# Two-level products one group earlier: the projection factor's second level prepared inside the first group's projection

## The chip, the cores and the metric

One core of one Trainium2 chip. The metric is device time in microseconds (us) of one execution; the median of several runs is compared. Engines are named as in the profile: PE is TensorE, DVE is VectorE, ACT is ScalarE, POOL is GpSimd, SP is SyncE, which here only issues transfers.

## The reference

An attention block without softmax feeds a gated feed-forward block, all in float32 (`w1` to `w_out` arrive as float64 and are converted on the chip).

```
kv  = einsum('bhsd,bhse->bhde', k, v)          # batch 8, heads 8, seq 576, head_dim 64
o   = einsum('bhsd,bhde->bhse', q, kv)
x   = o / sqrt(mean(o*o, -1) + 1e-6) * g_norm  # rows: 8 x 576 = 4608 tokens, 512 columns
a   = x @ w1                                   # 512 -> 1024
b   = x @ w2                                   # 512 -> 1024
out = ((a * b) @ w3) @ w_out                   # 1024 -> 1024 -> 512
```

## The kernel before

**Folded weights.** `w3 @ w_out` does not depend on the tokens, so the kernel first forms that 1024 x 512 matrix, `w3o_sb`, here called the projection factor (lines 664 to 686, the first 84 us). What is left for each token is: the gates `x @ w1` and `x @ w2`, their product, and one projection by `w3o_sb`.

**Groups.** Tokens are taken in nine groups of 512: T = 0 to 6 hold the first 512 tokens of batches 0 to 6, T = 8 the 64 left-over tokens of all eight batches, and T = 7 those of batch 7; they run in the order 0, 1, ..., 6, 8, 7. "First group" is T = 0, "second" T = 1, and so on. While group T is in its gates and projection, the attention of batch T + 1 is computed in pieces, set between the matmuls by `between()` (lines 1400 to 1418): each call takes one of eight pieces from `steps(T + 1)`. For an odd batch there is one product more, `product_left` (L431), for the left-over tokens of two batches.

**One level.** `winograd` (lines 695 to 735) multiplies two matrices, cut two by two, by seven half-size products instead of eight (the Strassen-Winograd scheme). It needs sums of blocks of the left factor (`sums`: s1 to s4) and differences of blocks of the right one (`combine`: t1 to t4). The gates take it once for each of four pairs of 128-column blocks, p = 0 to 3, for both `w1` and `w2`: 28 matmuls of 128 x 256 at L702 for one p. In the order of the code: the products a11 x b11, s1 x t1, s2 x t2, then `between`, s4 x b22 (block c12 is done), s3 x t3 (c22), a12 x b21 (c11), then `between`, a22 x t4 (c21). Products are collected in PSUM banks, five of which (`ps_mm`) go round; ACT copies (L715, `keep`) and DVE additions (L844, L845) finish the blocks. The copies u2 and u3 share one buffer, so u3 waits until the c12 addition has read u2; the last product is added to the bank that u3 copies, so it waits for u3.

**Two levels.** The same scheme can be used again inside each product. `project_twice` does so for the projection of every group but the first: 98 matmuls of 128 x 128 at L1169 for a group. The first group's projection, `project`, has one level (56 matmuls of 128 x 256 at L702). The factor for the second level is made once, by `prepare_b` (lines 1065 to 1091): seven steps n = 0 to 6, one for each block or block difference of `w3o_sb` (`b_blocks`: b11, t1, t2, b22, t3, b21, t4), each of four DVE subtractions of 128 x 256 (one of them in place) into a stage, and two stores to the DRAM buffer `w3o_l2`; one more store at the start keeps b21 as it was. Groups then load it part by part with `load_b`, in three buffers, `streams`, that lie over `w3o_sb` and the space of its differences; the second group's projection is the first to use it.

In the gates, `gates_of_two` (lines 932 to 1024) takes p = 0 and 1 together in two levels, 98 matmuls of 128 x 128 at L960, for the groups from `FIRST_OF_TWO` = 3 on, that is from the fourth; p = 2 and 3 stay with `winograd`. The second level's sums of the gate weights are made one group ahead, by `prepare_w` and `replace_a21` (lines 875 to 896), called from T = FIRST_OF_TWO - 1: 28 DVE instructions and 18 stores to the DRAM buffer `w_l2`; `load_w` brings them back in five parts for every group in two levels. Their stages (`in_a_row`, lines 798, 799 and 1514) lie in t1's space, in the last row of `w3o_sb` with the end of t4's space, and in a tile of their own.

**Turning.** Attention needs transposes of q and of its result. They go by DMA: a copy that splits the words (L293, L295), a DMA transpose (L297, issued by SP), a copy back (L307). POOL makes these copies up to batch FIRST_OF_TWO - 1, and ACT, in set places (`turns_by_scalar`), from batch FIRST_OF_TWO on.

**What sets the order.** PE, POOL and SP execute in the order in which the code issues. SP therefore also waits in that order: a store that waits for DVE holds back every transfer written after it. The order on DVE and ACT is made by the scheduler from estimated times, with the code's order as priority, except where the code fixes it by hand on DVE (the last gates pass and the projection of a group, and the two-level gates of the last two groups). `tc.issue_after(x)` only says that an instruction comes behind x on its own engine. Both execute their queue strictly in order once it is made.

`combine_x(T)` makes t1 to t4 of a group's x, in the buffer `xc` (and t3 in place). For T = 1 it is called after the first group's projection:

```
        project(T, between)
        run(combine_x(1))
        preparing, preparing_w, prepared, replaced = prepare_b(), prepare_w(), [], []
```

Of the kernel before, what the change touches and what calls it, by code (L numbers as in the profile page):

```python
# [22 lines left out]
def kernel(  # L23
# [32 lines left out]
    nc = tc.nc  # L56
    PSUM = bass.MemoryType.PSUM
    P = 128
# [3 lines left out]
    DF = w1.shape[1]  # L62
    NP = H // 2
    KF = DF // P
    FIRST_OF_TWO = 3
    NH = KF // 2
    J = 4
    G = J * P
# [46 lines left out]
    NF = KF // 2  # L115
# [576 lines left out]
    def late_tile(name):  # L692
        return late_pool.tile([P, 7, P], FP32, name=name[0] if name[0] == "u" else name)

    def winograd(lhsT, rhs, chunks, done, between=lambda: None, keep_u3=True):


        def product(a_name, b_name, to=None):
            ps = to if to is not None else bank(ps_mm, "mm").rearrange("p (u n) -> p u n", u=2)
            for u in range(2):  # L700
                for c in range(chunks):
                    nc.tensor.matmul(  # L702
                        ps[:, u, :],
                        lhsT=lhsT(a_name, u, c),
                        rhs=rhs(b_name, c),

                        start=(u == 0 and c == 0 and to is None),
                        stop=(c == chunks - 1),
                        skip_group_check=True,
                    )  # L710
            return ps

        def keep(name, ps):
            t = late_tile(name)[:, 0:4, :].rearrange("p (u a) n -> p u (a n)", u=2)
            copies.setdefault(name, []).append(nc.scalar.copy(t, ps))  # L715
            run_slot((stage[0], name), copies[name][-1])
            late[name] = t
            return t

        r1 = product("a11", "b11")  # L720
        p1 = keep("p1", r1)
        r2 = product("s1", "t1")
        p5 = keep("p5", r2)
        product("s2", "t2", r1)
        u2 = keep("u2", r1)
        between()
        product("s4", "b22", r2)
        done("c12", r2, u2)
        product("s3", "t3", r1)
        done("c22", p5, keep("u3", r1) if keep_u3 else r1)  # L730
        r3 = product("a12", "b21")
        done("c11", r3, p1)
        between()
        product("a22", "t4", r1)
        done("c21", r1, None)
# [297 lines left out]
            lambda: nc.vector.tensor_sub(s4, c21, s2),  # L1033
        ]

    def project(T, between):
        def done(name, one, two):
            half, j = int(name[1]) - 1, int(name[2]) - 1
            dst = o_sbs[half][:, :, j * N:(j + 1) * N]
            if two is None:  # L1040
                nc.scalar.copy(dst, one)
            else:
                nc.vector.tensor_add(dst, one, two)
            if name in ("c11", "c21"):
                rows = out[T * S:T * S + G, :].rearrange("(p j) f -> p j f", j=J)
                nc.sync.dma_start(out=rows[:, 2 * half:2 * half + 2, :], in_=o_sbs[half])

        winograd(
            lambda name, m, p: aa[p][name][:, m * P:(m + 1) * P],
            lambda name, p: ob[p][name],  # L1050
            NF, done, between,
        )


# [10 lines left out]
    def prepare_b():  # L1065

        nc.sync.dma_start(
            out=w3o_l2[7, :, 0:1024].rearrange("p (f n) -> p f n", n=N), in_=b_blocks()[5]
        )
        for n, y in enumerate(b_blocks()):  # L1070
            b11, b12, b21, b22 = (
                y[:, 2 * i:2 * i + 2, j * P:(j + 1) * P] for i in range(2) for j in range(2)
            )


            stage = w3o_sums[0].rearrange("p f n -> p (f n)") if n == 4 else (
                o_sbs[(n - n // 5) % 2].rearrange("p m n -> p (m n)")
            )
            stage = stage[:, 0:6 * P]
            t1, t2, t4 = (t.rearrange("p (c n) -> p c n", n=P) for t in (  # L1080
                stage[:, i * 2 * P:(i + 1) * 2 * P] for i in range(3)
            ))
            nc.vector.tensor_sub(t1, b12, b11)
            nc.vector.tensor_sub(t2, b22, t1)
            nc.vector.tensor_sub(b12, b22, b12)
            nc.vector.tensor_sub(t4, b21, t2)
            nc.sync.dma_start(
                out=w3o_l2[n, :, 0:1024].rearrange("p (f n) -> p f n", n=N), in_=y
            )
            nc.sync.dma_start(out=w3o_l2[n, :, 1024:PART], in_=stage)  # L1090
            yield
# [5 lines left out]
    def load_b():  # L1097
        n = len(loaded_b)
        if n == ALL_B:
            return  # L1100
        i = n % 7
        t = streams[n % 3] if n < 7 else streams[(i + 1 if i < 3 else i) % 3]
        if n >= 7 and i == 3:
            done_with = xT[groups[1 + n // 7]]
            t = done_with.rearrange("p i j r n -> p (i j r n)")[:, 0:PART]

        part = {ALL_B - 2: 6, ALL_B - 1: 7}.get(n, n % 7)

        queue = nc.scalar if i in ((3, 5) if n < 7 else (4, 6)) else nc.sync
        if n + 1 < ALL_B:  # L1110
            queue.dma_start(out=t, in_=w3o_l2[part])
        else:
            t = t[:, 0:1024]
            queue.dma_start(out=t, in_=w3o_l2[part, :, 0:1024])
        loaded_b.append(t)
# [275 lines left out]
    for n, T in enumerate(groups):  # L1391
# [8 lines left out]
        def between():  # L1400
            if len(converted) < len(begun):
                with tc.issue_after(copies["u2"][-1].ins):
                    end_next()
            next(pieces, lambda: None)()
            if T == FIRST_OF_TWO - 1 and p == 1 and len(prepared) == 1:
                with tc.issue_after(adds["c21"][-1].ins):
                    prepare_some(2)
            if T == 1:
                late_half = len(adds["c12"]) > len(adds["c21"])
                behind = adds["c21"][-1] if p else adds["norm"]  # L1410
                with tc.issue_after(behind.ins):
                    for _ in range((0 if late_half else 1) if p == 1 else 3 if p == 2 else 2):
                        if next(preparing, 0) == 0 and len(loaded_b) < 3:
                            load_b()
            if T == FIRST_OF_TWO - 1 and p == 2:
                replaced.append(True)
                if len(replaced) == 2:
                    replace_a21()
# [18 lines left out]
        for p in range(NF):  # L1437
# [23 lines left out]
            if T == 0:  # L1461

                def begin_early(behind):
                    t = early.pop(0)
                    with tc.issue_after(behind.ins):
                        next(t)
                    next(t)

                if p == 0:
                    begin_early(copies["xT"])  # L1470
                if p + 1 < NF:
                    ops = sum_w(p + 1)
                    if p != 2:
                        ops.pop(0)()
                    with tc.issue_after(adds["c12"][p].ins):
                        run(ops)
                for n in range(2):
                    if len(converted) < len(todo):
                        ahead = [copies["p5"][p] if p else copies["xT"], copies["u3" if p == 1 else "u2"][p]][n]
                        with tc.issue_after(ahead.ins):  # L1480
                            begin_next()
                        if len(begun) < len(todo):
                            with tc.issue_after(adds["c12"][0].ins):
                                end_next()
                if p == 0:
                    begin_early(copies["u3"][0])
                if p + 1 == NF:
                    allocate_projection()
                    first, *others = zip(*(f(i) for i in range(NF) for f in (sum_ab, combine_w3o)))
                    with tc.issue_after(adds["c21"][p - 2].ins):  # L1490
                        all_of(step() for step in first)
                    with tc.issue_after(adds["c12"][p - 1].ins):
                        all_of(step() for steps in others for step in steps)
            else:
                ops = [step() for step in sum_ab(p)]
                with tc.issue_after(ops[-1].ins):
                    if p == 1:
                        prepare_some(3)
                    if (T, p) == (1, 1):
                        all_of(preparing)  # L1500
        last = n + 1 == NG
        if T:
            project_twice(
# [2 lines left out]
            )  # L1506
            in_order.__exit__(None, None, None)
            continue
        project(T, between)
        run(combine_x(1))  # L1510
        preparing, preparing_w, prepared, replaced = prepare_b(), prepare_w(), [], []
        third = late_pool.tile([P, 3, 2, P], FP32, name="inner_sums")
        inner_sums.append([third[:, i] for i in range(3)])
        in_a_row.append({"s1": third.rearrange("p s c t -> p (s c t)")})
# [30 lines left out]
```

## Time and profile before

| | us |
|---|---|
| median of 3 runs | 749.06 |
| lowest, highest | 748.76, 749.10 |
| the profiled execution | 749.29 |
| its span, from the first to the last instruction | 747.5 |

| engine | busy us | share of the span | instructions |
|---|---|---|---|
| PE, matmuls | 740.4 | 99% | 6759 |
| PE, weight loads (beside matmuls) | 658.8 | 88% | 6759 |
| DVE | 639.6 | 86% | 1339 |
| ACT | 361.8 | 48% | 630 |
| POOL | 40.9 | 5% | 46 |

The profile is of one execution, the last two rows of the first table, and its sums are to be set against that execution's own time. The granted TensorE clock was 1.00. A line such as L702 is the line in the kernel's file. Names in the profile are those of the tiles: `raw` is the space that held the converted weights and later holds the differences of the projection factor, the stages and the outputs; `w3o_l` and `w_l` are the DRAM buffers of the two second levels; `ws` are the sums of the gate weights, `xc` and `xT` the tokens.

### The profile page before, as it was taken

The page shows a single profiled execution, that of the slowest core. Times are in us where ns is not written, and L with a number is a line of the kernel's source. Part 1 is how long each engine was busy: PE and PEld are TensorE (multiplying, and loading weights), DVE is VectorE, ACT ScalarE, POOL GpSimd, SP SyncE. Part 2 cuts the span into 40 slices and gives each one's busy share as a digit, 9 for nine tenths or more (in the row PEclk, how much of TensorE's full clock was granted, in tenths as well). Part 3 has the DMA queues.
Part 4 walks back from the last instruction along what each step waited for, and adds up shares of the span by engine and source line. Part 5 has one row for each costly group of instructions (what it writes and reads, how often), then busy time and mean ns, then how long its engine had stood idle before and what let it go on. Part 6 is the DMA issues. An engine that isn't in the chain of part 4 may idle for free.

```text
span 747.5 us, 16773 instructions
## 1 busy us (share of the span) xinstructions
PE 740.4 (99%) x6759; PEld 658.8 (88%) x6759; DVE 639.6 (86%) x1339; ACT 361.8 (48%) x630; POOL 40.9 (5%) x46
## 2 busy tenths in 40 slices
PE   8999999999999999999999999999999999999998
PEld 6455788888899889999999999999999999999997
DVE  6977998748889877988898989898989997898897
ACT  6687778413322565357636753565367323222321
POOL 0000000133330100010000000100001000000000
PEclk9999999999999999999999999999999999999999
DMA  9997925539998996677967997689659763465354
GB/s 313 361 310 208 265 93 133 125 83 265 278 311 301 277 286 167 228 229 211 305 227 220 228 275 263 209 240 283 234 133 243 203 222 100 154 225 172 130 197 140
DMA packets 134737, 165.32 MB, mean 221 GB/s; under 512 B 77956, under 2 KB 110724, under 8 KB 134660
## 3 DMA queue, kind: packets, MB, share of 16 engines
q1 hardware_dynamic: 132208, 149.84, 66.8%
q10 hardware_dynamic: 2452, 14.42, 5.6%
q8 instruction: 53, 0.87, 0.5%
q14 instruction: 24, 0.20, 0.1%
HBM read 126.22 MB, written 20.71 MB: 197 GB/s over the span
## 4 chain that ended last, share of the span: by engine, by line
PE 92%; DMA 3%; DVE 3%; ACT 1%; issue 0%; SPq 0%; ACTq 0%; DVEq 0%
PE mm L702 40%; PE mm L1169 22%; PE mm L960 18%; PE mm L681 5%; PE at L334 2%; DMA raw<-in_moe_w_dram 2%; PE at L412 1%; DMA raw<-in_moe_w_out_dram 1%; PE mm L412 1%; DMA w3o_sb<-w3o_l 1%; PE at L668 1%; DVE ab L162 1%; DVE w_sb L172 0%; PE at L1220 0%; ACT ab L158 0%
## 5 line engine op out<-in xcount | busy, mean ns | idle before, releaser
L702 PE MATMUL mm<-xT,w_sb 128*128 128x256 f32 x528 | 121.2, 379 | 0.0
L702 PEld LDWEIGHTS mm<-xT,w_sb 128*128 128x128 f32 x528 | 99.5, 190 | 13.5 <-issue 0.5
L702 PE MATMUL mm<-xc,ws 128*128 128x256 f32 x384 | 86.8, 379 | 0.0
L702 PEld LDWEIGHTS mm<-xc,ws 128*128 128x128 f32 x384 | 73.0, 190 | 9.9
L681 PE MATMUL mm<-chunks,ab 128*128 128x512 f32 x128 | 60.4, 604 | 0.7 <-DVE chunks L172 0.7
L715 ACT COPY u<-mm 128x512 f32<-128x512 f32 x42 | 24.6, 586 | 58.7 <-PE mm L702 41.2
L715 ACT COPY p<-mm 128x512 f32<-128x512 f32 x50 | 29.5, 589 | 45.5 <-PE mm L702 30.4
L1180 ACT COPY u<-mm 128x512 f32<-128x512 f32 x23 | 13.5, 586 | 77.8 <-DVE raw L1193 45.8
L1169 PE MATMUL mm<-w3o_sb,ab 128*128 128x128 f32 x368 | 48.7, 275 | 0.0
L1169 PE MATMUL mm<-w3o_sb,raw 128*128 128x128 f32 x372 | 48.1, 275 | 0.2 <-DMA w3o_sb<-w3o_l 0.2
L702 PE MATMUL mm<-xc,w_sb 128*128 128x256 f32 x192 | 46.4, 384 | 0.7 <-ACT u L715 0.7
L960 PE MATMUL mm<-ws,w3o_sb 128*128 128x128 f32 x300 | 46.2, 275 | 0.0
L1169 PEld LDWEIGHTS mm<-w3o_sb,ab 128*128 128x128 f32 x368 | 45.4, 192 | 0.4
L1169 PEld LDWEIGHTS mm<-w3o_sb,raw 128*128 128x128 f32 x372 | 44.7, 192 | 0.4 <-issue 0.4
L702 PE MATMUL mm<-xT,ws 128*128 128x256 f32 x176 | 42.3, 383 | 0.0
L681 PEld LDWEIGHTS mm<-chunks,ab 128*128 128x128 f32 x128 | 21.8, 190 | 23.3 <-issue 15.3
L380 DVE TENSOR_REDUCE inv<-sq 128x8 f32<-128x512 f32 (+1 forms) x40 | 24.3, 628 | 20.2 <-ACT sq L379 20.2
L702 PEld LDWEIGHTS mm<-xc,w_sb 128*128 128x128 f32 x192 | 35.7, 190 | 6.5 <-ACT u L715 1.5
L960 PEld LDWEIGHTS mm<-ws,w3o_sb 128*128 128x128 f32 x300 | 39.8, 192 | 0.0
L702 PEld LDWEIGHTS mm<-xT,ws 128*128 128x128 f32 x176 | 32.9, 190 | 4.7
L839 ACT COPY c<-mm 128x256 f32<-128x256 f32 x24 | 8.9, 370 | 57.0 <-PE mm L702 57.0
L845 DVE TENSOR_TENSOR ab<-c 128x256 f32<-128x256 f32 x72 | 32.5, 452 | 1.9
(244 smaller groups left out, 1685.5 us busy)
## 6 DMA issues: line engine op xcount, KB each, us to landing
w3o_sb<-w3o_l SPq DMA_DIRECT2D x18, 896.0 KB, 6.8
w3o_sb<-w_l SPq DMA_DIRECT2D x18, 896.0 KB, 6.1
raw<-in_moe_w_dram SPq DMA_DIRECT2D x31, 512.0 KB, 7.4
raw<-w3o_l SPq DMA_DIRECT2D x15, 896.0 KB, 4.8
w3o_sb<-w3o_l ACTq DMA_DIRECT2D x14, 896.0 KB, 5.2
k_sb<-in_k_dram SPq DMA_DIRECT2D x16, 576.0 KB, 4.5
v_sb<-in_v_dram SPq DMA_DIRECT2D x16, 576.0 KB, 6.3
q_sb<-in_q_dram SPq DMA_DIRECT2D x32, 256.0 KB, 3.7
```

The costliest lines, as they stand in the source:

```text
L162: nc.vector.scalar_tensor_tensor(out=low_bits, in0=hi, scalar=0x80000000, in1=low_bits, op0=ALU.bitwise_and, op1=ALU.bitwise_or,)
L334: nc.tensor.matmul(ps[r * D:(r + 1) * D, :], lhsT=k_sb[rows, r, cols], rhs=v_sb[rows, r, cols], start=(j == 0), stop=(j == JS - 1),)
L380: adds["norm"] = nc.vector.tensor_reduce(out=inv[:, i], in_=sq.rearrange("p (h d) -> p h d", d=D), axis=AX.X, op=ALU.add)
L412: nc.tensor.matmul(o_ps[l][tokens, n * D:(n + 1) * D], lhsT=qT[r][rows, e, i, tokens], rhs=kv_b[rows, m // 2 ^ l, e, h, :], start=True, st ...
L681: nc.tensor.matmul(sums_ps[half][m], lhsT=w3T[half, c][:, m, :], rhs=chunks[:, c, 1, :], start=(c == 0), stop=(c == KF - 1),)
L702: nc.tensor.matmul(ps[:, u, :], lhsT=lhsT(a_name, u, c), rhs=rhs(b_name, c),  start=(u == 0 and c == 0 and to is None), stop=(c == chunks ...
L715: copies.setdefault(name, []).append(nc.scalar.copy(t, ps))
L839: copied = nc.scalar.copy(c, one[:, 0, :])
L845: nc.vector.tensor_mul(dst, c[:, 0, :], c[:, 1, :])
L960: nc.tensor.matmul(ps[place // 4][:, place % 4, :], lhsT=x, rhs=y, start=new and place // 4 not in seen, stop=True, skip_group_check=True,)
L1169: nc.tensor.matmul(to[:, i, :], lhsT=x[:, c, :], rhs=y[:, c, :], start=new and place // 4 not in seen, stop=(c == 1), skip_group_check=True,)
L1180: nc.scalar.copy(t[:, 0:4], ps[0])
```

## The change

`FIRST_OF_TWO` goes from 3 to 2. So the third group's gates take p = 0 and 1 in two levels, the second group makes the sums of the gate weights for it (`prepare_w`, `replace_a21`), and ACT makes the turning copies of batch 2.

`prepare_b` leaves the second group, where it was set in portions between the passes. It is begun inside the first group's projection: a new argument `after` of `winograd` is called after each product's matmuls, and takes two steps of `prepare_b` after the fourth product and one each after the fifth and sixth. The other three steps come behind the projection. The stages change with it: n = 0 and 1 use `xc`, the others the space of the sums of `ab` (`ab_sums`). `combine_x(1)` is put behind the last addition of the projection's outputs on DVE. The first three loads of the projection factor in the second group are written at one place, at p = 2.

```diff
-    FIRST_OF_TWO = 3
+    FIRST_OF_TWO = 2
...
-    def winograd(lhsT, rhs, chunks, done, between=lambda: None, keep_u3=True):
+    def winograd(
+        lhsT, rhs, chunks, done, between=lambda: None, keep_u3=True, after=lambda: None,
+    ):
...
                         skip_group_check=True,
                     )
+            after()
             return ps
...
-    def project(T, between):
+    def project(T, between, after):
...
-                nc.vector.tensor_add(dst, one, two)
+                adds["out"] = nc.vector.tensor_add(dst, one, two)
...
-            NF, done, between,
+            NF, done, between, after=after,
...
-            stage = w3o_sums[0].rearrange("p f n -> p (f n)") if n == 4 else (
-                o_sbs[(n - n // 5) % 2].rearrange("p m n -> p (m n)")
-            )
-            stage = stage[:, 0:6 * P]
+            if n < 2:
+                stage = xc.rearrange("p s c n -> p (s c n)")[:, n * 6 * P:(n + 1) * 6 * P]
+            else:
+                stage = ab_sums[(n - 2) % 3].rearrange("p f n -> p (f n)")[:, 0:6 * P]
...
-            if T == 1:
-                late_half = len(adds["c12"]) > len(adds["c21"])
-                behind = adds["c21"][-1] if p else adds["norm"]
-                with tc.issue_after(behind.ins):
-                    for _ in range((0 if late_half else 1) if p == 1 else 3 if p == 2 else 2):
-                        if next(preparing, 0) == 0 and len(loaded_b) < 3:
-                            load_b()
+            if T == 1 and p == 2 and not loaded_b:
+                for _ in range(3):
+                    load_b()
...
-                    if (T, p) == (1, 1):
-                        all_of(preparing)
...
-        project(T, between)
-        run(combine_x(1))
-        preparing, preparing_w, prepared, replaced = prepare_b(), prepare_w(), [], []
+        preparing, calls = prepare_b(), []
+
+        def after():
+            for _ in range((0, 0, 0, 2, 1, 1, 0)[len(calls)]):
+                next(preparing)
+            calls.append(True)
+
+        project(T, between, after)
+        with tc.issue_after(adds["out"].ins):
+            run(combine_x(1))
+        all_of(preparing)
+        preparing_w, prepared, replaced = prepare_w(), [], []
```

## The prediction

> **What bounds the kernel now.** I read the busy table first, then the chain that ended last, by engine and in order of time, then windows of whole groups.
>
> ```profile
> span 747.5 us, 16773 instructions
> ...
> PE 740.4 (99%) x6759; PEld 658.8 (88%) x6759; DVE 639.6 (86%) x1339; ACT 361.8 (48%) x630; POOL 40.9 (5%) x46
> ...
> PE 92%; DMA 3%; DVE 3%; ACT 1%; issue 0%; SPq 0%; ACTq 0%; DVEq 0%
> ```
>
> TensorE is busy 99% of the span and carries 92% of the chain: a microsecond off its work, or added to it as a wait, is a microsecond of the kernel. The chain through the third group (T = 2) shows the work (start, duration, what; counts take matmuls and weight loads together):
>
> ```profile
> 240.17 10.36 PE mm L702 x48
> ...
> 252.67 19.19 PE mm L702 x88
> ...
> 274.00 5.38 PE mm L702 x24
> 279.38 0.62 PE at L431 x32
> 280.01 14.01 PE mm L702 x64
> 294.02 21.88 PE mm L1169 x196
> ```
>
> There is no gap: 112 matmuls of 256 columns at L702 in 48.94 us (10.36 + 19.19 + 5.38 + 14.01), the attention of batch 3 between them, 98 matmuls of 128 columns at L1169. The fifth group (T = 4) has the same odd kind of batch in its slots, but takes the gates of p = 0 and 1 in two levels:
>
> ```profile
> 403.31 9.38 PE mm L960 x84
> 412.69 0.62 PE at L431 x32
> 413.31 6.45 PE mm L960 x56
> 419.76 1.09 PE at L412 x64
> 420.85 6.45 PE mm L960 x56
> ```
>
> Here 98 matmuls at L960 (22.28 us) stand for 56 at L702. The windows of the second, third and fifth group (length; busy time of PE, PEld, DVE, ACT, POOL; clock; DMA share; GB/s):
>
> ```profile
> 164.55:240.17 75.62, 75.40 (x694) 68.74 (x693) 63.97 (x127) 20.80 (x47) 20.33 (x19) 1.00 1.00 292
> 240.17:315.90 75.73, 75.73 (x725) 68.90 (x725) 61.79 (x144) 39.71 (x68) 4.07 (x4) 1.00 0.77 231
> 388.88:462.68 73.80, 73.80 (x809) 69.83 (x809) 66.37 (x151) 41.79 (x74) 1.04 (x1) 1.00 0.83 245
> ```
>
> **What the Trainium skill says.** "FP8 and Floating Point Precision", TensorE Precision Notes, gives true FP32 four passes; "TensorE: Matmul & The Clock Gate", Back-to-back issue gap, gives an isolated warm matmul of N columns N/2.4 + 2.5 ns. Together that is 4 x (128/2.4 + 2.5) = 223 ns and 4 x (256/2.4 + 2.5) = 437 ns, estimates; the trace has 21.88/98 = 223 ns and 12.09/28 = 432 ns (a p-pass with no attention in it). So columns are what costs. "SBUF — State Buffer", Who interferes with whom: a VectorE instruction with two SBUF inputs contends with a GpSimd instruction that reads SBUF. The trace agrees: 256-column subtractions follow each other 0.34 us apart, and last 1.25 to 1.32 us while POOL copies (L1083 at 194.61, L755 at 189.80).
>
> **The change, part by part.**
>
> 1. *Third group in two levels.* Out go 56 matmuls x 432 ns = 24.18 us, in come 98 x 223 ns = 21.88 us: -2.30 us. Restarts around attention give some back, and the windows contain them: 73.80 - 75.73 = **-1.93 us**, which I take. The fifth group already does all that the third then does: 8 VectorE instructions of sum_x, 52 of gates_of_two and sum_ab_two where two p-passes have 22, and five weight loads (4.2 MB by the DMA list). PE has no idle time there, so they cost nothing; without that cover a load takes 6.1 us. Bounds: -2.30, and -1.5 if a load is late by some 0.4.
>
> 2. *Second group sums the gate weights.* The 28 VectorE instructions and 18 stores (4.2 MB) of prepare_w and replace_a21 move here from the third group, where they lay beside a full PE; batch 2's turning goes from POOL to ACT, as batch 3's does now. Most of prepare_b leaves. So this group should become the third of now without the left-over product: 75.73 - 0.62 = 75.11 for 75.62. The half microsecond in which it is now longer is one wait, for the projection's fourth factor (n = 3), loaded into streams[0] once products(0) has let it go:
>
> ```profile
> 217.74 3.14 PE mm L1169 x28
> ...
> 221.03 6.16 DMA w3o_sb<-w3o_l
> 227.19 0.14 issue
> 227.33 12.84 PE mm L1169 x112
> ```
>
> From 217.74 to 240.17 is 22.43 us for 98 matmuls that take 21.88 elsewhere: 0.55 lost. That load still starts 3.1 us into the projection. But it ran beside two transposes that SP issued at 220.14; by the slots of T = 2 these come at the fourth pass's u2 instead, some 7 us before. The 14 loads of its kind on ACT's queue have a median of 5.2 us, which would be in time. I take half: **-0.3**, bounds -0.55 and +0.4. The first three factors are loaded at p = 2, after the stores and ahead of need, as now (206.9).
>
> 3. *prepare_b in the first group's projection.* 28 VectorE instructions x 0.34 = 9.5 us and 15 stores (6.8 MB), from the second group to 144-170 us. The windows 139.5 to 164.55 have VectorE at 10.83 of 25.05 us; from 144.7 to 153.3 it stands still behind combine_x(1), which waits for POOL's xT. That wait goes, since combine_x now comes behind the last c11 addition (161.3). n = 0 and 1 fit in that hole, n = 2 and 3 before 161. POOL copies for 7.7 us of this window, so up to two thirds of that is lost to VectorE (0.34 for 1.25), 5 us; still 10.8 + 5.5 + 5 of 25. SP has x's two transposes at 146.8 and then nothing until 162.0, so the first nine stores go out early (DMA share 0.01 in 153.3:161.3). combine_x needs 4 x 0.6 = 2.4 us, so t1 is there at about 162.6 and t2 at 163.2, where PE wants them at 166.28 and 168: cost **0**, 3.7 us in hand. If the stores of n = 0 and 1, whose stage is xc, landed after 165, PE would stand for the rest; at the 4.5 to 5.2 us that they take now they land by 157.
>
> 4. *What is left at the second group's start.* After combine_x (164.4) VectorE has n = 4 to 6 (12 x 0.34 = 4.0, to 168.5), then prepare_w's first two names (6 x 0.34, of which POOL's copies from 168.9 to 172.6 make up to 4), and behind them the first c12 addition, ready at 171.5 and done from 173.50 now:
>
> ```profile
> 170.91 0.71 DVE L1083 TENSOR_TENSOR raw<-raw 128x256 f32<-128x256 f32 x1 [4.36 <-DMA out_dram<-raw]
> ...
> 173.50 0.68 DVE L844 TENSOR_TENSOR c<-mm,u 128x512 f32<-128x512 f32 x1
> ```
>
> This is the added wait. The second name's sums go into w3o_sb's last row and the end of t4's block, so they wait for the stores of blocks 5 and 6. SP issues these behind the output half and three transposes (162 to 168), six stores at about 0.6 us: to 171.8, landing 4.5 to 5.2 us later, 175 to 177. If the scheduler has put those sums ahead of c12, the addition, the copy u3 (same buffer as u2) and the product a22 x t4 queue up behind them. That product starts at 177.2, so c12 may begin as late as 177.2 - 0.6 - 0.7 = 175.9. VectorE then also owes the norm and c21 by 181. Now c12 comes 2 us late without any idle time of PE. Cost between 0 and 2; I take **0.2**. Below nothing it can't be, as PE doesn't stand there now. T = 1's loads of q, k and v behind these stores on SP come up to 4 us later (q now at 171.4), against uses from 181 on: nothing.
>
> Sum: -1.93 - 0.3 + 0 + 0.2 = -2.0 us. The profiled execution took 749.29 (span 747.5 and 1.8 around it), 0.23 above the median of 749.06; the sum makes it 747.3, and the median **747.0**.
>
> **Rivals.** *(a) Most of the gain is lost at the second group's start.* The sums stand ahead of c12 until 177: c12 1.1 us late, and c21's bank late by about as much again, so PE loses about 1.5 to 2. That gives 748.7. For it: VectorE is kept in order, it waited 4.36 us on a store at this very place, with c12 2 us late. Against it: the order is made from estimated times, and a store that lands late there lets c12 go first.
> *(b) Slower.* The same place, stores later: SP's six stores slide behind transposes in flight (two transposes held SP for 7.6 us at 180.81), block 6 lands at 181, c12 starts there, u3 is done at 182.3, the product starts 5.1 us late. 749.06 - 2.2 + 5.1 = 752.0. It decides from a c12 after 179.6 (175.9 + 2.2 + 1.5). For it: DMA share 1.00 in this group. Against: the group then moves no more than now (6.8 MB of w3o_l2's stores go mostly out, 4.2 MB come in), and 9 of the 15 are already done.
> *(c) The gates' saving isn't there,* since VectorE becomes the bound in a third group in two levels: the time would stay at 749. The fifth group's unbroken PE speaks against it; a few in a hundred, within (a).
>
> **How the numbers follow.** 0.2% (1.5 us) is about what a measurement of this kernel can tell from no change: 747.56 and 750.56 are the borders. The forecast holds 746.2 (-2.30 and -0.55) to 747.5; chance 0.60. Rival (a), 747.6 to 750.5: 0.28. Rival (b), above 750.6: 0.12. The forecast's own range is 746.2 to 747.6; the range that leaves out about 2 in 10 reaches through (a) to 749.8.
>
> **What would show it.** Right: a third group of 73.8 us with 98 matmuls at L960 and no wait before them; a second group near 75.1 with no or a shorter wait at the projection's fourth factor; the first group's projection still 25.0 from start to the second group, with prepare_b's VectorE work between 144 and 169. Wrong: PE idle at L702 with a release by an ACT copy of u or by VectorE within 166 to 186, where VectorE's wait before prepare_w's sums names a store to w3o_l.

## The result, and the profile after

| | before | after |
|---|---|---|
| median of 4 runs, us | 749.08 | 756.39 |
| lowest, highest | 748.76, 749.39 | 754.11, 756.90 |
| the profiled execution | 749.29 | 756.53 |
| its span | 747.5 | 754.8 |

The changed kernel is slower by 0.9%: ratio 1.0092, 95% interval 1.0071 to 1.0113. The forecast was 747.0 us, and 749.8 the upper end of its range. The busy table of after and its chain by engine:

```profile
span 754.8 us, 16987 instructions
...
PE 739.8 (98%) x6843; PEld 659.1 (87%) x6843; DVE 649.4 (86%) x1377; ACT 379.3 (50%) x652; POOL 21.8 (3%) x29
...
PE 74%; DMA 2%; SPq 1%; DVE 0%; ACT 0%; issue 0%; ACTq 0%; DVEq 0%
```

PE's busy time fell, from 740.4 to 739.8, although part of it (below) ran at half speed. The span grew by 7.3. So PE stands where it did not stand before. The windows of the second and third group show where (length; busy PE, PEld, DVE, ACT, POOL; clock; DMA share; GB/s):

```profile
164.47:249.16 84.69, 77.91 (x694) 69.38 (x693) 60.16 (x139) 36.71 (x63) 3.64 (x5) 0.98 0.92 263
249.16:322.96 73.80, 73.80 (x809) 69.84 (x809) 65.62 (x149) 41.77 (x74) 1.11 (x1) 1.00 0.82 241
```

The third group is now 73.80 us, as the fifth was, 1.93 less than its 75.73. The second grew from 75.62 to 84.69, by 9.07. The first part up to 164.47 is 0.08 shorter. The groups from the fourth on have the lengths of before, but the time behind PE's last matmul is 3.4 us for 3.2, as in every kernel here with `FIRST_OF_TWO` = 2; why is not shown. 9.07 - 1.93 - 0.08 + 0.2 = 7.3 us. The chain through the third group has the gates in two levels (L963; 84 + 56 + 56 records, for the fifth's 84 + 56 + 56) and, from 249.16 on, no gap:

```profile
263.59 9.38 PE mm L963 x84
...
301.07 21.88 PE mm L1172 x196
```

Everything that is to be explained lies in the second group. PE's timeline there, only the entries with idle time (start, duration; in brackets the idle time ahead and its releaser):

```profile
167.08 3.69 PE L704 MATMUL mm<-xc,ws 128*128 128x256 f32 x16 [0.72 <-DVE xc L748]
...
186.61 1.99 PE L704 MATMUL mm<-xc,ws 128*128 128x256 f32 x8 [3.14 <-ACT p L718]
189.38 1.99 PE L704 MATMUL mm<-xT,ws 128*128 128x256 f32 x8 [0.77 <-ACT p L718]
...
202.15 3.68 PE L704 MATMUL mm<-xc,ws 128*128 128x256 f32 x8 [2.15 <-ACT p L718]
```

Four waits, 6.8 us together, of the 9.5 by which the gates of this group grew (62.70 us from 164.47 to the projection's start at 227.17, for 53.19). Most of the rest is lost speed: the last line takes 3.68 us for the work of 1.73, 1.95 more. What is left, 0.8, would be the restarts after the four waits, 0.2 each; that is an estimate. A window of just the slow stretch gives the granted clock, 0.54:

```profile
202.15:205.83 3.68, 3.68 (x12) 2.55 (x14) 2.44 (x8) 1.49 (x2) 0.00 (x0) 0.54 0.97 309
```

Three of the waits are put down to a copy by ACT of a product bank (`keep`, now L718). But ACT is more than half idle in this group (36.71 of 84.69 us busy). What held it is read from ACT's own timeline:

```profile
185.78 0.31 ACT L384 ACTIVATE inv<-inv,eps_col 128x16 f32<-128x16 f32 x1 [5.35 <-DVE inv L380]
186.00 0.56 ACT L718 COPY p<-mm 128x512 f32<-128x512 f32 x1
187.79 1.04 ACT L295 COPY qT<-q_sb 128x1024 uint16<-128x1024 uint16 x1 [1.23 <-DMA q_sb<-in_q_dram]
188.74 0.58 ACT L718 COPY p<-mm 128x512 f32<-128x512 f32 x1
...
200.45 1.16 ACT L307 COPY xT<-xn 128x1024 uint16<-128x1024 uint16 x1 [0.32 <-DMA xn<-xT]
201.52 0.58 ACT L718 COPY p<-mm 128x512 f32<-128x512 f32 x1
```

Each late copy stands directly behind something that PE does not need yet, but that was itself waiting: the square root of batch 2's norm (L384), which had waited 5.35 us for DVE; then a turning copy of q (L295), waiting for a load; then turning copies (L307), waiting for transposes. ACT takes its queue in order, so the copy waits too. One more step back, DVE's timeline:

```profile
161.98 0.43 DVE L1086 TENSOR_TENSOR raw<-w3o_sb 128x256 f32<-128x256 f32 x1 [3.57 <-DMA w3o_l<-raw]
...
164.17 0.43 DVE L1086 TENSOR_TENSOR raw<-raw 128x256 f32<-128x256 f32 x1 [0.25 <-DMA w3o_l<-raw]
...
166.25 0.68 DVE L748 TENSOR_TENSOR xc<-xT 128x512 f32<-128x512 f32 x1
...
172.60 0.69 DVE L847 TENSOR_TENSOR c<-mm,u 128x512 f32<-128x512 f32 x1 [2.40 <-PE mm L704]
...
179.38 0.43 DVE L884 TENSOR_TENSOR w3o_sb<-w_sb 128x256 f32<-128x256 f32 x1 [2.55 <-DMA w3o_l<-w3o_sb]
181.97 0.43 DVE L758 TENSOR_TENSOR raw<-ab,ab 128x256 f32<-128x256 f32 x1 [1.49 <-DMA w3o_l<-raw]
...
184.13 0.42 DVE L759 TENSOR_TENSOR raw<-raw,ab 128x256 f32<-128x256 f32 x1 [0.52 <-DMA w3o_l<-raw]
184.47 1.27 DVE L380 TENSOR_REDUCE inv<-sq 128x8 f32<-128x512 f32 x2
```

Every wait here but that for PE is for a store of `prepare_b` (`w3o_l<-...`) to let go of its source. At 161.98 the sixth step of `prepare_b` (n = 5) wants the stage of n = 2, whose store is still out. It and the seventh (164.17) stand in DVE's queue ahead of the outputs' last addition and of `combine_x(1)` (L748, at 166.25), and PE waits 0.72 for the latter. `prepare_w` has seven steps of three sums each, here called names, one for each product. At 179.38 the second name writes the last row of `w3o_sb`, still being stored. At 181.97 the sums of `ab` for p = 0 (L758, and L759 to 184.5) write into `ab_sums`, where the stages now are, and wait twice. Behind all of them stands the norm's reduction, and behind that, on ACT, PE's next copy. The chain, in order of time, joins the three engines:

```profile
176.64 6.53 DMA w3o_l<-raw
183.19 0.44 DVE raw L886
183.64 0.36 SPq L876
...
184.09 3.60 DMA q_sb<-in_q_dram
```

So a store issued at 176.64 takes 6.53 us, holds DVE until 183.19 (the second name's last sum, L886), thereby SP's next store (L876), and behind this one the load of q. SP's timeline, the line of before first, then that of after:

```profile
171.36 1.68 SPq L95 DMA_DIRECT2D q_sb<-in_q_dram  x2
184.09 0.96 SPq L95 DMA_DIRECT2D q_sb<-in_q_dram  x2
```

That load is what ACT waits for at 187.79, and the transposes behind it are the ones that ACT waits for at 197.65 and 200.45.

### The profile page after: what moved, and what is told of

Read it like the earlier page. It is cut to its first block, busy times and chain, and to the rows that moved or that the text cites. A ratio compares the mean times of both kernels' runs of the same rounds, so it can differ in the third digit from the quotient of the medians.

```text
span 754.8 us, 16987 instructions
## 1 busy us (share of the span) xinstructions
PE 739.8 (98%) x6843; PEld 659.1 (87%) x6843; DVE 649.4 (86%) x1377; ACT 379.3 (50%) x652; POOL 21.8 (3%) x29
## 4 chain that ended last, share of the span: by engine, by line
PE 74%; DMA 2%; SPq 1%; DVE 0%; ACT 0%; issue 0%; ACTq 0%; DVEq 0%
PE mm L704 27%; PE mm L1172 23%; PE mm L963 21%; PE at L334 2%; PE at L412 1%; DMA w3o_l<-raw 1%; PE mm L412 1%; DMA q_sb<-in_q_dram 0%; PE at L1223 0%; SPq L297 0%; DMA xn<-xT 0%; PE at L431 0%; DVE c L847 0%; ACT u L718 0%; ACT p L718 0%
## 5 line engine op out<-in xcount | busy, mean ns | idle before, releaser
L704 PE MATMUL mm<-xT,w_sb 128*128 128x256 f32 x480 | 110.2, 379 | 0.0
L704 PEld LDWEIGHTS mm<-xT,w_sb 128*128 128x128 f32 x480 | 90.3, 190 | 12.2 <-issue 0.5
L704 PE MATMUL mm<-xc,ws 128*128 128x256 f32 x352 | 81.9, 385 | 6.0 <-ACT p L718 5.3
L704 PEld LDWEIGHTS mm<-xc,ws 128*128 128x128 f32 x352 | 67.7, 193 | 16.5 <-ACT p L718 6.1
L963 PE MATMUL mm<-ws,w3o_sb 128*128 128x128 f32 x350 | 53.9, 275 | 0.0
L718 ACT COPY u<-mm 128x512 f32<-128x512 f32 x38 | 22.2, 585 | 56.5 <-PE mm L704 38.3
L718 ACT COPY p<-mm 128x512 f32<-128x512 f32 x46 | 27.0, 587 | 42.1 <-PE mm L704 26.9
L963 PEld LDWEIGHTS mm<-ws,w3o_sb 128*128 128x128 f32 x350 | 46.4, 192 | 0.0
L704 PE MATMUL mm<-xc,w_sb 128*128 128x256 f32 x176 | 42.5, 384 | 0.7 <-ACT u L718 0.7
L704 PE MATMUL mm<-xT,ws 128*128 128x256 f32 x160 | 38.6, 384 | 0.8 <-ACT p L718 0.8
L704 PEld LDWEIGHTS mm<-xc,w_sb 128*128 128x128 f32 x176 | 32.7, 190 | 6.0 <-ACT u L718 1.4
L704 PEld LDWEIGHTS mm<-xT,ws 128*128 128x128 f32 x160 | 29.7, 190 | 5.4 <-ACT p L718 1.2
L307 ACT COPY xT<-xn 128x1024 uint16<-128x1024 uint16 x28 | 32.5, 1167 | 0.8 <-DMA xn<-xT 0.8
```

The lines of the kernel that those rows point to most:

```text
L307: copy(words(dst), src)
L704: nc.tensor.matmul(ps[:, u, :], lhsT=lhsT(a_name, u, c), rhs=rhs(b_name, c),  start=(u == 0 and c == 0 and to is None), stop=(c == chunks ...
L963: nc.tensor.matmul(ps[place // 4][:, place % 4, :], lhsT=x, rhs=y, start=new and place // 4 not in seen, stop=True, skip_group_check=True,)
```

## The experiments

At first two explanations stood against each other: `prepare_w`'s sums, standing in DVE's queue behind late stores, and the turning of batch 2, which the change gives to ACT. Medians and ratios are against runs of the kernel before on the same chip (medians 748.85 to 749.08). A profile shows one execution; where that lies far from the median of its kernel, it is said.

| kernel | median us (lowest to highest) | ratio to before, 95% interval |
|---|---|---|
| e1_prep_b_alone | 754.51 (754.27 to 755.12) | 1.0077 [1.0062, 1.0092] |
| e2_late_w | 754.78 (753.86 to 755.23) | 1.0077 [1.0062, 1.0092] |
| e3_pool_turn | 762.49 (762.08 to 763.50) | 1.0184 [1.0169, 1.0199] |
| e4_no_reuse | 751.19 (749.13 to 753.33) | 1.0028 [1.0013, 1.0042] |
| e11_b_alone_third | 749.26 (748.40 to 749.68) | 1.0002 [0.9994, 1.0011] |
| e5_late_w_no_reuse | 751.32 (749.66 to 754.76) | 1.0040 [1.0021, 1.0059] |
| e9_late_w_third | 753.30 (752.40 to 753.77) | 1.0056 [1.0041, 1.0071] |
| e10_two_levels_alone | 763.51 (762.66 to 763.76) | 1.0190 [1.0173, 1.0207] |
| e13_one_two_four | 749.73 (747.82 to 750.79) | 1.0004 [0.9996, 1.0012] |
| e14_none_three_four | 749.36 (748.34 to 750.98) | 1.0000 [0.9987, 1.0012] |
| e15_spread | 749.91 (747.59 to 751.96) | 1.0009 [0.9999, 1.0019] |
| e16_spread_steady | 749.55 (748.47 to 752.85) | 1.0011 [1.0003, 1.0019] |
| e17_no_w_stores | 748.01 (747.25 to 749.74) | 0.9988 [0.9981, 0.9995] |

**e1: the changed kernel with prepare_b's move alone.**

```diff
-    FIRST_OF_TWO = 2
+    FIRST_OF_TWO = 3
```

> prepare_b in the first group's projection alone, with FIRST_OF_TWO back at 3. Theory Q (the loss is a queue: in the second group the sums of the gate weights on DVE, the q loads on SP and with them ACT's copies stand behind prepare_b's last stores): with no prepare_w in the second group only combine_x's 0.9 us stays, against the 0.55 that the projection's wait gives back: about 749.4. Rival D (prepare_b's 6.8 MB in the first projection are too much by themselves, wherever prepare_w lies): 753 or more.

754.51: most of the loss is there with no `prepare_w` in this group and batch 2 turned by POOL. Both explanations fail as the main one. The time fits rival D, the traffic of the stores alone; e4 and e11 decide against it. PE waits 0.74 us for `combine_x` (166.87) and 3.21 for an ACT copy of p (186.47). The chain of this kernel leads to the second wait:

```profile
177.58 6.38 DMA w3o_l<-raw
183.99 0.43 DVE raw L759
...
185.85 0.57 ACT p L718
```

The sums of `ab` (L759) wait for the store of a stage, issued at 177.58, and the norm and ACT's copy stand behind. The third explanation is therefore the place of the stages: `ab_sums` is taken twice by `prepare_b` itself (n = 5 and 6 after n = 2 and 3), and is wanted by the second group for its first sums of `ab`.

**e2: the first two names of prepare_w only at the end of p = 0.**

```diff
-        if T == FIRST_OF_TWO - 1:
-            with tc.issue_after(adds["out"].ins):
-                prepare_some(2)
...
-                    if p == 1:
-                        prepare_some(3)
+                    if p < 2:
+                        prepare_some((2, 3)[p])
```

> The change, with prepare_w's first two names moved from the start of the second group to the end of its first pass (behind sum_ab of p = 0), so that DVE doesn't wait there for the stores of blocks 5 and 6, and SP has the q loads ahead of these sums' stores. Theory Q: the stalls in p = 1 (3.3 + 0.8 us) and in p = 2 (2.15 + 1.95 at half the clock) go, combine_x's 0.9 stays: about 748.2. Rival T (it is the turning of batch 2 on ACT that holds PE): the stalls in p = 2 stay, about 752.

754.78. Waits of 0.92 (for `combine_x`) and 3.92 (ACT's copy) stay, the chain again going through a 6.78 us store and the sums of `ab`. The wait in p = 2 and its slow clock are gone, with batch 2's turning still on ACT. Its load of q is issued at 179.16, 4.9 us earlier than in after, while PE comes there 1.5 us later. So that wait came with the late load of q, not with ACT's work as such.

**e3: batch 2's turning copies back on POOL.**

```diff
-        by_scalar, in_two = b >= FIRST_OF_TWO, b > FIRST_OF_TWO
+        by_scalar, in_two = b > FIRST_OF_TWO, b > FIRST_OF_TWO
```

> The change, with the turning copies of batch 2 left to POOL (by_scalar from batch 3 on, as before the change). Theory Q: ACT no longer waits for q's loads and transposes ahead of a p copy, so 0.8 + 2.15 + 1.95 us go; the square root that waits for DVE still stands ahead of the p1 copy, so 3.3 + 0.9 stay: about 751.5. Rival T: all but combine_x's 0.9 goes: about 748.5.

762.49, against every expectation. The waits at the group's start stay (1.07 and 3.07), and new ones follow: 6.66 us at 215.56 for ACT's copy of u, behind a chain of POOL's copies, a 9.18 us pair of transposes, SP's next store of `w_l` and DVE's sums; and 1.14 at 235.41, where two sums of `ab` take 1.38 us each beside a POOL copy instead of 0.42. In this kernel ACT is the better place for these copies.

**e4: the stages of n = 5 and 6 in a buffer of their own** (the tokens of batch 0, no longer needed).

```diff
+            elif n < 5:
+                stage = ab_sums[n - 2].rearrange("p f n -> p (f n)")[:, 0:6 * P]
             else:
-                stage = ab_sums[(n - 2) % 3].rearrange("p f n -> p (f n)")[:, 0:6 * P]
+                stage = xT[0].rearrange("p i j c n -> p (i j c n)")[:, (n - 5) * 6 * P:(n - 4) * 6 * P]
```

> The change, with stages n = 5 and 6 in the first group's xT instead of ab_sums a second time, so that no stage is written twice and DVE doesn't wait 3.6 us for the store of n = 2 ahead of the c22 and c11 additions and combine_x. Theory Q: the 0.9 us at combine_x go, the last stores land some 3 us earlier, and with them the sums and the q loads: 752 to 753.5. Rival D: it stays at 755 or more, since the transfers take as long.

751.19, 5.2 us less than the changed kernel, from two buffers. The wait for `combine_x` is gone (L748 at 161.80), so it was made by the second use of the stage of n = 2. Left in the profiled execution, the slowest of the five (753.33), are 0.85, 0.83 and 2.23 us, and the chain now does go through `prepare_w`:

```profile
174.37 6.47 DMA w3o_l<-raw
180.86 0.44 DVE raw L886
```

That is the second name's sum, waiting for block 6's store, the place that the prediction had named.

**e11: e1 with all three late stages elsewhere** (n = 4 in the tile `inner_sums`, n = 5 and 6 as in e4).

```diff
-    FIRST_OF_TWO = 2
+    FIRST_OF_TWO = 3
...
+            elif n == 4:
+                stage = third.rearrange("p s c t -> p (s c t)")
```

> prepare_b in the first group's projection alone (FIRST_OF_TWO = 3) as in e1, with the late stages out of ab_sums: n = 4 in inner_sums' tile, n = 5 and 6 in the first group's xT. Theory S (DVE stands in order behind stores of stages in ab_sums: n = 5 and 6 behind those of n = 2 and 3, and the second group's own sums of ab behind those of n = 4 to 6): all of e1's loss goes and the projection's 0.55 stays won, about 748.3. Rival D (the stores are too much traffic there): 751 or more.

749.26, equal to before, and no wait of PE in the gates of the second group. Its chain where after and e1 have their gaps (177 to 218) is TensorE alone:

```profile
177.43 19.19 PE mm L704 x88
196.62 1.21 PE at L334 x72
198.76 19.19 PE mm L704 x88
```

All of e1's loss, 5.3 us by the medians, was the stages; the 6.8 MB of stores are the same in both. Moving `prepare_b` as such costs nothing that can be measured, and this group takes 240.13 - 164.77 = 75.4 us for 75.62, begun 0.2 later. The 748.3 that was expected does not come: part of the projection's 0.55 is still lost (22.2 us for 21.88).

**e5 and e9: e2's late prepare_w, with e4's stages (e5), and with e11's (e9).** No edit beyond those shown.

> The change with both: prepare_w's first two names at the end of the second group's first pass (as e2), and stages n = 5 and 6 in the first group's xT (as e4). Theory S: combine_x's 0.9 us and the waits of the sums of ab for the stages of n = 5 and 6 go; what may stay is up to 2 us for the stage of n = 4 and for q's turning in p = 2: 746.8 to 748.8. Rival Q alone (only the order on SP counts): as e4 or e2, 751 to 755.

> As e5, with the stage of n = 4 in inner_sums' tile too, so that no stage late in ab_sums is left. Theory S: the third group's 1.93 and the projection's 0.55 are won and nothing stays lost: 746.6 to 747.2. If ACT's waits for q's loads and transposes hold PE by themselves, some 4 us stay: 750.5.

751.32 and 753.30. Both miss what theory S had; e5's number lies in the rival's range, but by another path. With the names so close together `prepare_w` now trips over its own stages. The chain of e5:

```profile
181.09 7.75 DMA w_l<-raw
188.86 0.44 DVE raw L884
```

The fourth name takes the stage of the first, whose store lasts 7.75 us (8.86 in e9). The profiled execution of e5 is the fastest of its seven (749.66; the slowest took 754.76). The c12 addition (190.42) stands behind it, then u3 (191.11), then PE (191.75), for 2.31 us (3.35 in e9). This is the path by u3 that the prediction drew.

**e10: two levels in the third group, prepare_b left at its old place.** This is the kernel before with

```diff
-    FIRST_OF_TWO = 3
+    FIRST_OF_TWO = 2
...
-            if T == FIRST_OF_TWO - 1 and p == 1 and len(prepared) == 1:
+            if T == FIRST_OF_TWO - 1 and p == 2 and not prepared:
...
-                    prepare_some(2)
+                    prepare_some(4)
...
+                    prepare_some(3)
                     replace_a21()
```

and without its other two calls of `prepare_some`.

> The kernel before with FIRST_OF_TWO = 2 alone: prepare_b stays in the second group's first two passes, and prepare_w with replace_a21 comes behind it, in p = 2. The third group should still win 1.93 us; the second group's DVE gets 9.5 us more in its last 40 us, of which some 7 are free (14.6 of 19.2 busy in p = 2 and 3, 21.4 of 22.5 in the projection). Theory S has no waits for stores in it, so 747 plus up to 3: 748 to 750. If DVE's work binds, 752.

763.51. The third group is 73.8 us again, but the second takes 256.38 - 164.91 = 91.5: PE waits 4.89 us in p = 1 behind transposes that SP issues late, and 6.18 at the projection's start, where DVE had first waited 7.58 us for a store of `w_l`. With `prepare_w` at these places, `prepare_b` must leave if it is to come; other places were not tried.

**e13 and e14: e4, with prepare_w's seven names in other portions,** 1, 2, 4 and 0, 3, 4 for the three places where after has 2, 2, 3.

> As e4 (stages n = 5 and 6 in the first group's xT), and of prepare_w only the first name at the second group's start (its stage is t1's space, stored long before), two names in p = 1 and four behind it. Theory S (DVE queues in order behind a store whose buffer it needs): the second name's sums no longer wait for the stores of blocks 5 and 6, and no stage of prepare_w is taken again while its store is under way, as it was in e5 and e9. Nothing is left but waits of ACT for q's transposes (q's loads at 178): 746.6 to 748.0. Rival T (ACT's waits for q's loads and transposes hold PE by themselves): 750 or more, with a stall in p = 2 as in e4.

> As e13, with no name at the start: three names in p = 1's first half (three different stages) and four behind it, so that q's loads stand on SP right behind prepare_b's stores (about 176, as in e5). Theory S: 746.6 to 747.5, if the 9 sums at once don't make c12 of p = 1 late (they take 3.0 us; c12 has about 3 in hand). Rival T: as e13, but less, since the loads are 2 us earlier: 748 to 749.

749.73 and 749.36: no difference from before, and both above what was expected. In e14's profile the third group is 73.80, but the second 241.81 - 164.47 = 77.3, with waits of 0.70, 0.41 and 0.38 us. What the third group gains, the second gives back all but 0.2. The rest by which this execution (750.19) is longer than that of before lies elsewhere: 1.0 us in the group T = 6, which the change does not touch, and the 0.2 at the end. In e13's profile (750.79, the slowest of its 13) the waits are 1.85 (ACT's copy behind a turning copy of q), 0.61 (the projection's last factor) and, in the third group, 0.66: there the fourth factor's load into `xT` takes 9.55 us, and the group 74.69.

**e15 and e16: spread further** (0, 2, 2 and 3 in p = 2; e16 also loads the fourth factor of the projection early, into the buffer that later groups use for it).

> As e14 (no stage of prepare_b taken twice, no weight sums at the second group's start), with prepare_w's seven names spread: two in p = 1's first half, two behind p = 1, three in p = 2's first half. Theory S: a stage of prepare_w is taken again some 10 us after its store instead of at once, so DVE's 0.7 to 1.9 us waits for w_l stores go and with them the two stalls (0.70 and 0.41): the second group 1 us shorter than e14's, about 748.2. If DVE's work in p = 2 binds instead (9 more instructions, 3 us), no gain: 749.4.

> As e15, and the second group loads its projection factor as the later groups do: n = 3 into the group's own xT ahead of the projection, and streams in their order, so that no load waits for products(0) to let its buffer go. Theory S: the projection's wait (0.4 to 0.6 us, with 0.1 around it) goes too: 747.6 or less, the third group's 1.93 us then stand nearly alone, and the kernel is faster than before by 0.1 to 0.3%. If the wait is for DMA traffic and not for the buffer: as e15.

749.91 and 749.55, with single runs from 747.59 to 752.85. In e15's profile PE waits 0.34 and 1.38 us in the gates, the longer one behind DVE's wait for a store of `w_l`, and the third group takes 74.37. In e16's profile (751.63, 2.1 above its median) the stores of `w_l` take 2.8 to 12.2 us (median 5.9), the fourth factor's load is issued only at 222.05, behind them and two pairs of transposes, and PE waits for it:

```profile
229.88 4.99 PE L1174 MATMUL mm<-xT,raw 128*128 128x128 f32 x28 [2.49 <-DMA xT<-w3o_l]
```

In a window over p = 3 (204 to 220) the DMA engines are full (share 1.05, 323 GB/s). That later stores only meet the projection's loads is argued from this one execution. It also shows something else: the gates take 53.03 us (164.76 to 217.79 in PE's timeline; in before 164.55 to 217.57) without any wait of PE, with the sums, their stores and ACT's turning of batch 2 all in this group. So none of the three has to cost PE there; what this execution loses, it loses in the projection (26.3 us for 21.88).

**e17: e14 without prepare_w's 18 stores.** It leaves out what the two-level gates need: `w_l2` is filled once from `w3o_sb` as the first group begins, so the gates multiply by other values.

```diff
-        nc.sync.dma_start(out=dst[:, :, at:at + src.shape[2]], in_=src)
+        if n < 0:
+            nc.sync.dma_start(out=dst[:, :, at:at + src.shape[2]], in_=src)
...
+    flat = w3o_sb.rearrange("p f n -> p (f n)")
+    for a in range(0, len(BLOCKS) * P, 4096):
+        c = min(4096, len(BLOCKS) * P - a)
+        nc.sync.dma_start(out=w_l2[:, a:a + c], in_=flat[:, 0:c])
```

> As e14, with the 18 stores of the gate weights' sums (4.2 MB in the second group) left out; w_l2 is filled once from w3o_sb at the first group's start instead, so the two-level gates multiply by other values, in the same time. All DVE work, ACT's turning of batch 2 and all loads stay. If what e14 still loses in its second group (77.2 us for 75.1) is those stores, as traffic, as places on SP's queue and as stages that DVE waits for: a second group of 75.0 to 75.5 us, and with a third of 73.8 about 747.0, plus what the fill costs the first group. Rival T (ACT's turning of batch 2): a second group of 76.5 or more.

748.01, 1.0 under before and 1.35 under e14; by the two ratios to before it is 0.9, and e14's interval is as wide as that on either side. So the stores, by their bytes, their places on SP's queue and their hold on the stages, which this run does not tell apart, are about half of what e14 still loses against the forecast's 747.0. With DVE's 28 sums left in, PE still waits, in its profile, 0.49 and 0.40 us for ACT's copies behind turning copies, first of q, then of batch 2's result. This execution (749.14) is 1.1 above its median; its second group takes 241.34 - 164.52 = 76.8 us, which is rival T's number.

No kernel here beats before with the whole computation in it.

## Why the prediction was wrong

**Step 1, the third group, -1.93: right.** 73.80 was forecast and 73.80 measured, in after and in nine of the eleven experiments with two levels there. In e13 and e15 it is 74.69 and 74.37, by a late load, the loss that the step gave as its bound (there the projection's fourth factor).

**Step 2, the second group.** Its projection went from 22.43 to 21.99 us, so the wait for the fourth factor went, -0.44, inside the bounds of -0.55 and +0.4. In part this may be luck: in e9, e13 and e14, whose second groups are shorter than that of after, PE waits 1.16, 0.61 and 0.38 us for the last factor instead. "This group should become ... 75.11" failed by 9.6, through steps 3 and 4.

**Step 3, "cost 0, 3.7 us in hand": the first step that failed,** by 0.9 (a wait of 0.72 and the restart). The step counted DVE's time for the 28 instructions, which did fit, but of the stages it priced only those in `xc`. Steps n = 5 and 6 take the stages of n = 2 and 3 again, and the diff says so: `ab_sums[(n - 2) % 3]`. The nine first stores were to go out early. They did, from 149.83, but filled the DMA engines (share 1.02 from 150 to 160), seven of them at 1.0 to 1.4 us of SP each, and the store of n = 2 held DVE for 3.57 us up to 161.98. The order was another, too: "After combine_x (164.4) VectorE has n = 4 to 6", but the scheduler put n = 4 and 5 and three of the four subtractions of n = 6 ahead of it, so DVE stood there before `combine_x`, which came at 166.25, not 162. e4 shows the cause: without that second use the wait is gone.

**Step 4, "between 0 and 2; I take 0.2": the term that was mis-sized,** by about 8. It had the right cause, stores of `prepare_b` landing late and DVE waiting in order. Its times were too early: it had the stores of blocks 5 and 6 landing at 175 to 177, rival (b) that of block 6 at 181, and DVE waited for them until 179.38 and 183.19. SP issued the six stores from 172.63 on, about 1.06 us apart and not 0.6, and the one that DVE waited for last took 6.53 us to land. It also had the wrong victim. c12 was not held: it ran at 172.60, earlier than before, since the scheduler put the sums behind it. Behind the sums stood the norm, and the step stopped at "VectorE then also owes the norm and c21 by 181", without asking who queues behind the norm: ACT's next copy of a bank, so PE. It also left out that the sums of `ab`, there in every version, write where the stages are; e1 and e11 show that this and the second use are 5.3 us. And "T = 1's loads of q ... against uses from 181 on: nothing" is refuted: the load came 12.7 us later, not 4, and the copies of q stand ahead of PE's copies in ACT's queue. That is the waits of 0.77 and 2.15 and the slow 1.95 after the latter; e2, with earlier loads, has neither wait.

**The rivals.** Rival (b), slower by a store that lands late at this place, was right in kind and given 0.12. Its time, 752.0, was 4.4 too low, as it followed one path to PE, by c12 and u3. That path exists (e5, e9), but in after PE was reached by the norm and by q. Of the signs named as "wrong", DVE's wait for a store to `w3o_l` is there, and so is a release by VectorE (167.08); the releaser of the longest wait is an ACT copy of p, not of u.

**A reading to correct.** The counts in the chain are not "matmuls and weight loads together". They count records of matmuls, two for each float32 matmul of the code. Durations per matmul are not touched by that.

**Where the expected 2 us went,** step by step: 756.39 with the stages as changed; 751.19 with two of them elsewhere; 749.36 with `prepare_w` later; 748.01 without its stores. The forecast's 747.0 is 1.0 further on. For this last 1.0 us the profile of e17 shows two waits behind turning copies on ACT, 0.9 together, and 0.1 more behind PE's last matmul. No run took that turning away from ACT without giving it to POOL, and in e16's profile the same turning costs PE nothing; so where the last 1.0 us go stays open.

## What to carry to other kernels

When stores are moved, price the release of each source buffer: who writes it next, and when the store lands with the DMA engines full. Then follow the waiting instruction's queue to its end, and the queues of those who wait in it; here a sum that nobody needed soon held a norm that nobody needed soon, and ahead of PE's copy that cost 3 us. A diff that replaces one stage index by another can be worth more than the arithmetic that the change is about (5.2 us against 1.93).

## What the runs showed of the hardware that was not expected

A short stand of PE can cost twice, and it need not. These are single waits of PE at L704 (L702 in e10), with the granted clock of the stretch right behind them, of 2 to 5 us:

| idle time, us | run | granted clock behind it |
|---|---|---|
| 2.15 | after | 0.54 |
| 2.23 | e4 | 0.67 |
| 2.31 | e5 | 1.00 |
| 3.07 | e3 | 1.00 |
| 3.14 | after | 1.00 |
| 3.21 | e1 | 0.54 |
| 3.35 | e9 | 0.54 |
| 3.92 | e2 | 0.67 |
| 4.89 | e10 | 0.50 |
| 6.66 | e3 | 0.50 |

The Trainium skill ("TensorE: Matmul & The Clock Gate", Part 1: The HAM clock gate) has the clock halved after at least one idle window of about 3.4 us, in windows that run freely. That nearly the same idle time has different consequences agrees with free windows; that 2.15 us can be enough does not agree with a whole idle window. No rule was found in these runs.

A store's time to landing is no constant. The 384 KB stores `w3o_l<-raw` have a median of 5.9 us in after, 5.2 in before; single stores of `w_l` took 7.75 (e5), 8.86 (e9) and 12.2 us (e16), with a DMA share of 1.15, 1.15 and 1.02 meanwhile. The price to use for a buffer's release is that of the stretch to which the store is moved.
